# FFT mixing and a gated feed-forward: transfers with 24 rows outermost, radix-2 sums on GpSimd behind the first mix half, and a 72-row matmul for the last groups

## The chip, the cores and the metric

The kernel runs on one core of one Trainium2 chip. The metric is the device time of one launch in microseconds (us). TensorE is called PE, VectorE DVE, ScalarE ACT, GpSimd POOL, and SyncE, which issues almost all transfers of this kernel in order, SP.

## The reference

```python
X = np.fft.rfft(x, axis=1)                      # x: 8 transforms, 3072 points, 256 channels
Yr = Xr @ w_r - Xi @ w_i + b_r                  # complex 256 x 256 mix of each frequency
Yi = Xr @ w_i + Xi @ w_r + b_i
Y = soft_threshold(Yr, 0.01) + 1j * soft_threshold(Yi, 0.01)
y = np.fft.irfft(Y, n=3072, axis=1)             # 24576 tokens of 256
out = ((y @ w_a) * (y @ w_b)) @ w_out           # 256 -> 1536 -> 256
```

## The kernel before

The feed-forward takes most of TensorE's time. It walks over 32 pairs of 384 tokens each way (4 quarters `q` for each of the 8 transforms `b`) and, in each, over 12 steps `j` of the hidden dimension (`step`). A step makes seven products of a Strassen scheme (`ych`, `ycl` with weights `wc`), which ScalarE copies out of PSUM (`s`, L1097; `g`) and VectorE adds up, and then the projection (`g` with `wo`). All operands are split into a high and a low part, so that a product is three matmuls.

Between the matmuls of a step stand two **slots**. A slot takes one task from a list, and the tasks are the Fourier stages of the *next* transform, so that they run in the shadow of the feed-forward:

- **f1** (13 units `u`, in the first quarter): `f1_load` brings a tile `xin` of 5 groups of 24 rows, ScalarE casts it to the high part (`x<-xin`, L469), GpSimd subtracts to get the low part, TensorE multiplies with the constants `c_sb`, ScalarE copies the result out (`gst`, L351), and SP stores it to the scratch `g_d`. `f1_pre` issues the load of unit u+3 and the cast of unit u+2 when unit u runs.
- **f2** (12 units): `mid_load` brings two rows of `g_d` (`gt`); their sum and difference are `gs`; TensorE multiplies them with `m_in`. Then comes a chain that prepares the mix: ScalarE copies (`xs`, L351) and casts (`sx`, L702), GpSimd or VectorE subtracts (`sx`, 512 elements a row), adds (`xs`, 256), ScalarE casts (L705), and GpSimd or VectorE subtracts again (`sx`, 256).
- **f3** (two halves of a unit): the complex mix, `sx` with `wm_h`, `wm_l`. The first half needs the 512-element `sx` at once, the cast L705 at its seventh matmul and the last `sx` at its ninth. Behind the second half VectorE builds `zy` and the clipped `zc`, GpSimd subtracts (`zy`), ScalarE casts (`zh`), GpSimd subtracts (`zl`).
- **i1**: `zh`, `zl` with `v_sb`; ScalarE copies to `dst`, and the sum and difference of its halves, `dto`, are stored to the scratch `d_d`.
- **i2** (four parts a quarter): `i2_load` brings `dt` (5 groups of 24 rows) and, in two of the four parts, `dl` (2 groups of 24, 48 rows); TensorE multiplies them with `t_in`; the results become the `ych`, `ycl` of the next pair of token groups.

The order of a unit's tasks is f3, f3, f2 of the next unit, i1 of the unit before, so four slots, two steps, a unit. `Order` is a planner that keeps model times for the engines and writes each engine's instructions in the order in which the model finds them ready; operations marked "GV" go to GpSimd unless the model finds that much too late, "VG" and "AV" likewise. `need` makes sure that a chain is written before the matmul that reads it. On the chip each engine runs its own list in order. The sum and difference `gs` are written by `mid_load`, `dto` by `i1`, whenever the model finds them ready:

```python
            ready = od.chain(
                ("GV", D, lambda e: tt(e, both[:, 0], t[:, 0], t[:, 1], ALU.add)),
                ("GV", D, lambda e: tt(e, both[:, 1], t[:, 0], t[:, 1], ALU.subtract)),
                after=ready,
            )
```

Of the kernel before, what the change touches and what calls it, by code (L numbers as in the profile page):

```python
# [43 lines left out]
def _constants():  # L44
# [72 lines left out]
    b1h, b1l = _split(b1.reshape(RB, (G + 1) * KT))  # L117
# [22 lines left out]
    b2 = np.zeros((G, KT, NPAIR, 6, G, M1))  # L140
    e2 = np.zeros((2, KT, NPAIR, 2, M1))
    for q in range(NPAIR):
        for h in range(G):
            for j in range(6):
                b2[h, :, q, j, h] = back[32 * q + 6 * h + j]
        for h in range(2):
            e2[h, :, q, h] = back[32 * q + 30 + h]
# [11 lines left out]
        "b1": np.ascontiguousarray(np.stack([b1h, b1l], 1)),  # L159
# [3 lines left out]
        "e2": e2.reshape(2 * KT, NPAIR * 2 * M1).astype(np.float32),  # L163
# [162 lines left out]
def fft_mix_glu_kernel(ctx: ExitStack, tc: tile.TileContext, x, w_r, w_i, b_r, b_i, w_a, w_b, w_out, c1f, vf, m2, v, t2, c3, b1, m2b, vz, b2, e2, out):  # L326
# [45 lines left out]
    c1_sb = const.tile([RB, 2, RB + KT], F32R, name="c1_sb")  # L372
# [53 lines left out]
    def split_mix():  # L426
        w2, w3, v_in = (p1.tile([P, 2, D], F32, tag=t, name="w_in") for t in ("sxh", "sxl", "xs"))
        v_in = v_in.rearrange("p s (i n) -> p s i n", i=2)
        c1_in = state["tmp"].tile([RB, 2, RB + KT], F32, name="c1_in", bufs=1)
# [3 lines left out]
        for q, bq in enumerate((b_r, b_i)):  # L433
# [4 lines left out]
            ("AV", 2 * (RB + KT), lambda e: copy(e, c1_sb, c1_in)),  # L438
# [101 lines left out]
    def out_weights(j):  # L540
# [29 lines left out]
    def f1_load(b, u):  # L570
        if b:
            t = p3.tile([RB, 512], F32, tag="ld", name="xin")
            xv = x[b].rearrange("(p m n) d -> m p (n d)", p=M1, n=2)
            if u < 6:
                nc.sync.dma_start(t, xv[u : u + 4 * STEP + 1 : STEP])
            else:
                nc.sync.dma_start(t[M1:], xv[u : u + 3 * STEP + 1 : STEP])
                nc.sync.dma_start(t[:M1], xv[min(u + 4 * STEP, 63)])
# [6 lines left out]
    def f1_pre(b, u):  # L585
# [6 lines left out]
        xs[b, u] = xh, xl, od.chain(*split(512, xi, xh, xl), after=t if b < 2 else 0.0)  # L592
# [28 lines left out]
    def f1_later(b, u):  # L621
        if u == 0:
            g_d[b] = dram.tile([KT, P * D], F32, tag="g_d", name="g_d")
# [3 lines left out]
        at = KT * (u >= 6)  # L627
        mm3(ps[:RB], c1_sb[:, 0, at : at + RB], c1_sb[:, 1, at : at + RB], xh, xl, True, True)
        g = p2.tile([RB, 512], F32, tag="st", name="gst")
        n = 5 if u + 4 * STEP < 64 else 4  # L630
        to = g_d[b].rearrange("s (m e) -> m s e", e=512)[u : u + (n - 1) * STEP + 1 : STEP]
        c = od.chain(
            ("AV", 512, lambda e: copy(e, g, ps[:RB])),
            ("S", 0, lambda e: nc.sync.dma_start(to, g[: n * KT])),
# [20 lines left out]
    def mid_load(b, u):  # L655
# [8 lines left out]
        ready = od.load(3 * P)  # L664
        both = p3.tile([P, 2, D], F32, tag="ld", name="gs") if u else t
        if u:
            ready = od.chain(
                ("GV", D, lambda e: tt(e, both[:, 0], t[:, 0], t[:, 1], ALU.add)),
                ("GV", D, lambda e: tt(e, both[:, 1], t[:, 0], t[:, 1], ALU.subtract)),
                after=ready,  # L670
            )
        gt[b, u] = both, m, ready

    def f2(b, u):
# [3 lines left out]
        elif u:  # L678
            od.need(t)
# [66 lines left out]

    f3_ps = {}
    zs_done = []

    def f3_plain(u, i):  # L750
# [33 lines left out]
        z = p1.tile([P, 2, D], F32, tag=("zy", "zc")[u % 2], name="zc")  # L784
# [16 lines left out]
    def f3(b, u, i):  # L801
# [17 lines left out]
        if i == 0:  # L819
# [11 lines left out]
            f3_ps[b, u] = bk, k, od.chain(*ops, urgent=1)  # L831
            return
# [369 lines left out]
    with tc.manual_schedule():  # L1202
# [140 lines left out]
```

## Time and profile before

| | |
|---|---|
| runs | 2970.67, 2972.41, 2974.66 us (median 2972.41) |
| profiled execution | 2974.97 us; its span, first to last instruction, 2973.2 us |
| PE | 2878.7 us busy, 97% of the span |
| DVE | 1909.4 us, 64% |
| ACT | 1446.4 us, 49% |
| POOL | 925.7 us, 31% |
| mean granted TensorE clock | 0.990 |
| chain that ended last | PE 75%, DMA 5%, ACT 5%, POOL 4%, issue 3%, DVE 3% |

Matmuls overlap each other in the profile, so a busy PE may still start its matmuls late; the share of the chain is what was followed back from the last instruction. The profiled execution took 2.6 us more than the median of the runs.

### The profile page before, as it was taken

How to read it: one execution, taken by the hardware profiler on the slowest of the kernel's cores; microseconds unless marked ns; L12 is line 12 of the kernel's file. 1: busy time of each engine (PE TensorE's matmuls, PEld its weight loads, DVE VectorE, ACT ScalarE, POOL GpSimd, SP SyncE). 2: the span in 40 equal slices, each digit the busy share in tenths (PEclk: the TensorE clock that was granted, in tenths of full speed). 3: DMA queues.
4: the chain of work that ended last, by engine and by line, in shares of the span. 5: the costliest groups of instructions: out<-in, count | busy, mean ns of one | idle time of the engine just before them, and what ended most of it. 6: DMA issues, size and time to landing. Idle time of an engine off the chain costs nothing.

```text
span 2973.2 us, 47139 instructions
## 1 busy us (share of the span) xinstructions
PE 2878.7 (97%) x16879; PEld 2666.9 (90%) x16879; DVE 1909.4 (64%) x3790; ACT 1446.4 (49%) x3212; POOL 925.7 (31%) x922
## 2 busy tenths in 40 slices
PE   7899999999999999999999999999999999999999
PEld 3589999899989999889998999989999899999998
DVE  7666666566755667556665666656666566666665
ACT  5554445545455444544445454454444544444444
POOL 1123433234422334224333243333342234420000
PEclk8899999999999999999999999999999999999999
DMA  7431212212122011321113111222112211110000
GB/s 244 136 101 41 58 36 83 83 41 62 37 98 81 29 57 40 108 72 41 47 48 110 57 59 33 60 100 59 54 36 63 99 56 56 39 46 27 27 11 22
DMA packets 130596, 190.08 MB, mean 64 GB/s; under 512 B 14389, under 2 KB 87473, under 8 KB 130361
## 3 DMA queue, kind: packets, MB, share of 16 engines
q1 hardware_dynamic: 128409, 179.55, 19.4%
q0 software_dynamic: 1840, 7.48, 0.8%
q8 instruction: 132, 2.16, 0.3%
q14 instruction: 103, 0.84, 0.1%
q10 hardware_dynamic: 112, 0.04, 0.0%
HBM read 111.52 MB, written 75.50 MB: 63 GB/s over the span
## 4 chain that ended last, share of the span: by engine, by line
PE 75%; DMA 5%; ACT 5%; POOL 4%; issue 3%; DVE 3%; SPq 1%; ACTq 0%; POOLq 0%; DVEq 0%
PE bank L360 75%; DMA xin<-in_x_dram 4%; ACT s L1097 2%; POOL sx L354 2%; DVE bank L354 1%; DMA gt<-g_d 1%; POOL gs L354 1%; POOL dto L354 1%; POOL xs L354 1%; DVE s L354 1%; POOL zl L354 0%; ACT x L469 0%; DVE zy L354 0%; ACT ych L469 0%; ACT xs L351 0%
## 5 line engine op out<-in xcount | busy, mean ns | idle before, releaser
L354 DVE TENSOR_TENSOR bank<-bank,s 128x384 f32<-128x384 f32 x1152 | 647.5, 562 | 608.7 <-PE bank L360 493.2
L1097 ACT COPY s<-bank 128x384 f32<-128x384 f32 x1152 | 550.0, 485 | 206.4 <-PE bank L360 202.0
L1134 ACT CAST g<-bank 128x384 fp32r<-128x384 f32 x384 | 184.6, 481 | 808.5 <-DVE s L354 412.3
L354 DVE TENSOR_TENSOR g<-bank,g 128x384 fp32r<-128x384 f32 x768 | 425.6, 556 | 195.3 <-ACT g L1134 158.4
L354 DVE TENSOR_TENSOR s<-bank,s 128x384 f32<-128x384 f32 x768 | 423.0, 551 | 8.4 <-issue 1.0
L354 POOL TENSOR_TENSOR ycl<-yr,ych 128x384 fp32r<-128x384 f32 x186 | 194.8, 1068 | 719.9 <-ACT ych L469 719.9
L1072 ACT CAST g<-bank 128x384 fp32r<-128x384 f32 x384 | 185.0, 482 | 214.5 <-DVE bank L354 213.9
L360 PE MATMUL bank<-ych,wc0l 128*128 128x384 f32 x672 | 237.3, 353 | 17.8 <-ACT s L1097 17.7
L354 POOL TENSOR_TENSOR zy<-zy,zc 128x512 f32<-128x512 f32 x77 | 99.0, 1286 | 468.0 <-DVE zc L850 468.0
L360 PE MATMUL bank<-ych,wc1l 128*128 128x384 f32 x672 | 233.3, 347 | 9.4 <-ACT s L1097 8.8
L360 PE MATMUL bank<-ych,wc3l 128*128 128x384 f32 x672 | 235.5, 351 | 1.4 <-ACT s L1097 1.0
L360 PE MATMUL bank<-ych,wc2l 128*128 128x384 f32 x672 | 235.0, 350 | 1.1 <-DVE s L354 0.9
L354 POOL TENSOR_TENSOR x<-xin,x 120x512 fp32r<-120x512 f32 x88 | 118.0, 1344 | 375.6 <-ACT x L469 213.4
L360 PE MATMUL bank<-ycl,wc0h 128*128 128x384 f32 x672 | 229.2, 341 | 0.0
L360 PE MATMUL bank<-ych,wc0h 128*128 128x384 f32 x672 | 229.1, 341 | 0.0
L360 PE MATMUL bank<-ycl,wc2h 128*128 128x384 f32 x672 | 226.5, 337 | 0.0
L360 PE MATMUL bank<-ycl,wc3h 128*128 128x384 f32 x672 | 226.4, 337 | 0.0
L360 PE MATMUL bank<-ycl,wc1h 128*128 128x384 f32 x672 | 226.3, 337 | 0.0
L360 PE MATMUL bank<-ych,wc1h 128*128 128x384 f32 x672 | 226.2, 337 | 0.0
L360 PE MATMUL bank<-ych,wc2h 128*128 128x384 f32 x672 | 226.2, 337 | 0.0
L360 PE MATMUL bank<-ych,wc3h 128*128 128x384 f32 x672 | 226.1, 336 | 0.0
L360 PE MATMUL bank<-wm_h,sx 128*128 128x256 f32 x1008 | 196.6, 285 | 12.9 <-POOL sx L354 12.8
(210 smaller groups left out, 6699.7 us busy)
## 6 DMA issues: line engine op xcount, KB each, us to landing
out_dram<-osb SPq DMA_DIRECT2D x64, 384.0 KB
g_d<-gst SPq DMA_DIRECT2D x84, 240.0 KB
dt<-d_d SPq DMA_DIRECT2D x56, 360.0 KB
gt<-g_d SPq DMA_DIRECT2D x154, 128.0 KB
d_d<-dto SPq DMA_DIRECT2D x154, 128.0 KB
xin<-in_x_dram SPq DMA_DIRECT2D x65, 192.0 KB
m_in<-const_m2b_dram SPq DMA_DIRECT2D x84, 128.0 KB
xin<-in_x_dram SPq DMA_DIRECT2D x42, 240.0 KB
```

The lines of the kernel that those rows point to most:

```text
L354: (nc.vector if e == "V" else nc.gpsimd).tensor_tensor(o, a, b, op=op)
L360: nc.tensor.matmul(o, lhsT=l, rhs=r, start=start, stop=stop, **kw)
L1072: ("A", W, lambda e: nc.scalar.copy(h, X)),
L1097: return s, od.chain(("A", W, lambda e: nc.scalar.copy(s, q[:, :W])), urgent=1)
L1134: ("A", W, lambda e: nc.scalar.copy(h1, Y)),
```

## The change

Five things are edited. (1) The tiles of f1 and i2 change their row order from (group, row) to (row, group), and the DRAM side of their transfers has the 24 rows as its outermost dimension in place of the 5, 4 or 2 groups; each f1 load is now two transfers in all 13 units, and the row of the scratch `g_d` is padded so that all units store 5 groups. The constants `b1`, `b2`, `e2` are reordered to match. (2) The last groups' matmul takes three groups, 72 rows, the first of which meets zero weights. (3) The sums `gs` of unit u+1 and `dto` of earlier units are written by `halves` directly behind the first mix half of unit u; `zc` shares the buffer of the low part of `sx`. (4) The list of f1 tasks leaves a slot empty after two units, before every third. (5) The cast of an f1 tile is written no earlier than the model's landing time, in all transforms and not in the first two alone.

```diff
-    e2 = np.zeros((2, KT, NPAIR, 2, M1))
+    b2 = np.zeros((KT, G, NPAIR, 6, G, M1))
+    e2 = np.zeros((KT, 3, NPAIR, 2, M1))
...
-            e2[h, :, q, h] = back[32 * q + 30 + h]
+            e2[:, h + 1, q, h] = back[32 * q + 30 + h]
...
-            xv = x[b].rearrange("(p m n) d -> m p (n d)", p=M1, n=2)
-            if u < 6:
-                nc.sync.dma_start(t, xv[u : u + 4 * STEP + 1 : STEP])
-            else:
-                nc.sync.dma_start(t[M1:], xv[u : u + 3 * STEP + 1 : STEP])
-                nc.sync.dma_start(t[:M1], xv[min(u + 4 * STEP, 63)])
+            xv = x[b].rearrange("(p m n) d -> p m (n d)", p=M1, n=2)
+            at, one = (u + STEP, u) if u < 6 else (u, min(u + 4 * STEP, 63))
+            nc.sync.dma_start(t[: 4 * M1], xv[:, at : at + 3 * STEP + 1 : STEP])
+            nc.sync.dma_start(t[4 * M1 :], xv[:, one])
...
-        xs[b, u] = xh, xl, od.chain(*split(512, xi, xh, xl), after=t if b < 2 else 0.0)
+        xs[b, u] = xh, xl, od.chain(*split(512, xi, xh, xl), after=t)
...
-        at = KT * (u >= 6)
-        mm3(ps[:RB], c1_sb[:, 0, at : at + RB], c1_sb[:, 1, at : at + RB], xh, xl, True, True)
+        c1u = c1_sb[:, int(u >= 6)]
+        mm3(ps[:RB], c1u[:, 0], c1u[:, 1], xh, xl, True, True)
         g = p2.tile([RB, 512], F32, tag="st", name="gst")
-        n = 5 if u + 4 * STEP < 64 else 4
-        to = g_d[b].rearrange("s (m e) -> m s e", e=512)[u : u + (n - 1) * STEP + 1 : STEP]
+        to = g_d[b].rearrange("s (h m e) -> s h m e", h=G, e=512)[:, :, u]
         c = od.chain(
             ("AV", 512, lambda e: copy(e, g, ps[:RB])),
-            ("S", 0, lambda e: nc.sync.dma_start(to, g[: n * KT])),
+            ("S", 0, lambda e: nc.sync.dma_start(to, g)),
...
-        ready = od.load(3 * P)
         both = p3.tile([P, 2, D], F32, tag="ld", name="gs") if u else t
-        if u:
-            ready = od.chain(
-                ("GV", D, lambda e: tt(e, both[:, 0], t[:, 0], t[:, 1], ALU.add)),
-                ("GV", D, lambda e: tt(e, both[:, 1], t[:, 0], t[:, 1], ALU.subtract)),
-                after=ready,
-            )
-        gt[b, u] = both, m, ready
+        gt[b, u] = both, m, t
...
-            od.need(t)
+            od.need(state["halves"])
...
             od.put(state["x"])
+            od.put(state["z"], 2 * (u > 1))
...
+    def halves(o, i, *then):
+
+        return od.chain(
+            ("GV", D, lambda e: tt(e, o[:, 0], i[:, 0], i[:, 1], ALU.add)),
+            ("GV", D, lambda e: tt(e, o[:, 1], i[:, 0], i[:, 1], ALU.subtract)),
+            *then,
+        )
...
+            if u < 11:
+                both, _, t = gt[b, u + 1]
+                state["halves"] = halves(both, t)
+            while later:
+                later.popleft()()
...
-        z = p1.tile([P, 2, D], F32, tag="zc", name="zc")
...
+        z = p1.tile([P, 2, D], F32, tag="sxl", name="zc")
...
+        if b and u > 1:
+            od.put(state["dto"])
...
-            ops = [
-                ("AV", 512, lambda e: copy(e, d, ps)),
-                ("GV", D, lambda e: tt(e, to[:, 0], d[:, 0], d[:, 1], ALU.add)),
-                ("GV", D, lambda e: tt(e, to[:, 1], d[:, 0], d[:, 1], ALU.subtract)),
-                ("S", 0, lambda e: mid_move(d_d[b], u, to, True)),
-            ]
-        c = od.chain(*ops, urgent=len(ops) if u == 11 or b == 0 else 1)
-        od.reads(bk, c, len(ops) - 1)
-        if u == 11:
-            (od.put if b else od.need)(c)
+            ops = [("AV", 512, lambda e: copy(e, d, ps))]
+
+            def last():
+                state["dto"] = halves(to, d, ("S", 0, lambda e: mid_move(d_d[b], u, to, True)))
+
+        c = od.chain(*ops, urgent=len(ops))
+        if b == 0 or u == 0:
+            od.reads(bk, c, 1)
+        else:
+            od.reads(bk, c, 0)
+            if u < 10:
+                later.append(last)
+            else:
+                od.put(c)
+                last()
+                if u == 11:
+                    od.put(state["dto"])
+        if b == 0 and u == 11:
+            od.need(c)
...
-        src = dv[:, :30].rearrange("s (h j) d -> h s j d", j=6)[:, :, 3 * th : 3 * th + 3]
+        src = dv[:, :30].rearrange("s (h j) d -> s h j d", j=6)[:, :, 3 * th : 3 * th + 3]
         nc.sync.dma_start(
-            t.rearrange("p n d -> p (n d)"), src.rearrange("h s j d -> h s (j d)")
+            t.rearrange("p n d -> p (n d)"), src.rearrange("s h j d -> s h (j d)")
         )
         cut = [(t[:, n], m[:, n * RB : (n + 1) * RB]) for n in range(3)]
         if th == 0:
-            last = p2.tile([2 * KT, D], F32, tag="dl", name="dl")
-            nc.sync.dma_start(m[: 2 * KT, T3:], e2[:, 2 * KT * q : 2 * KT * (q + 1)])
-            nc.sync.dma_start(last, dv[:, 30:].rearrange("s h d -> h s d"))
-            cut.append((last, m[: 2 * KT, T3:]))
+            last = p2.tile([3 * KT, D], F32, tag="dl", name="dl")
+            nc.sync.dma_start(m[: 3 * KT, T3:], e2[:, 2 * KT * q : 2 * KT * (q + 1)])
+            nc.sync.dma_start(last, dv[:, 29:])
+            cut.append((last, m[: 3 * KT, T3:]))
...
-                        work += f1_tasks(b + 1)[0 if b else AHEAD :]
+                        ts = f1_tasks(b + 1)[0 if b else AHEAD :]
+                        for i in range(0, len(ts), 3):
+                            work += [*ts[i : i + 2], None, *ts[i + 2 : i + 3]]```

GpSimd's list at the beginning of a transform's third quarter, from the fifth unit's `zy` to the last `sx` of the sixth unit, in the kernel before (a row is an operation, its tiles and its shape):

```order
L354 TENSOR_TENSOR zy<-zy,zc 128x512
L354 TENSOR_TENSOR zl<-zy,zh 128x512
L354 TENSOR_TENSOR gs<-gt 128x256
L354 TENSOR_TENSOR sx<-xs,sx 128x2x256
L354 TENSOR_TENSOR gs<-gt 128x256
L354 TENSOR_TENSOR xs<-xs 128x2x128
L354 TENSOR_TENSOR sx<-xs,sx 128x2x128
```

The `gs` in it belong to a later unit. The same place in the changed kernel, from the sums behind the fifth unit's first mix half:

```order
L355 TENSOR_TENSOR gs<-gt 128x256
L355 TENSOR_TENSOR dto<-dst 128x256
L355 TENSOR_TENSOR gs<-gt 128x256
L355 TENSOR_TENSOR dto<-dst 128x256
L355 TENSOR_TENSOR zy<-zy,zc 128x512
L355 TENSOR_TENSOR zl<-zy,zh 128x512
L355 TENSOR_TENSOR sx<-xs,sx 128x2x256
L355 TENSOR_TENSOR xs<-xs 128x2x128
L355 TENSOR_TENSOR sx<-xs,sx 128x2x128
```

Nothing stands between `zl` and the last `sx` any more but the chain itself, and the four sums stand ahead of `zy`. The 42 `xs` and 35 last `sx` that VectorE did are now GpSimd's, as are all 154 `gs` and all 154 `dto`. In one unit of each transform a `ycl` stands between `xs` and the last `sx`, and in one five `ycl` stand ahead of the sums.

SP's list in the f1 stage of the kernel before (a store of `g_d`, then the two transfers of a load; the shape is that of the written side):

```order
L634 DMA g_d<-gst 5x24x512
L577 DMA xin<-in_x_dram 96x1x512
L578 DMA xin<-in_x_dram 24x512
L634 DMA g_d<-gst 5x24x512
L577 DMA xin<-in_x_dram 96x1x512
L578 DMA xin<-in_x_dram 24x512
```

The 96-row load reads 4 groups of 24 rows here. The same stretch of SP's list in the changed kernel:

```order
L632 DMA g_d<-gst 120x512
L576 DMA xin<-in_x_dram 96x1x512
L577 DMA xin<-in_x_dram 24x512
L632 DMA g_d<-gst 120x512
L576 DMA xin<-in_x_dram 96x1x512
L577 DMA xin<-in_x_dram 24x512
```

The order is the same; the store is one dimension of 120 rows, and the read side of the 96-row load, which these rows don't print, is 24 rows of 4 groups.

## Rows read from the trace of the kernel before

**Rows 1.** The page, busy time, share and instructions of each engine.
```profile
PE 2878.7 (97%) x16879; PEld 2666.9 (90%) x16879; DVE 1909.4 (64%) x3790; ACT 1446.4 (49%) x3212; POOL 925.7 (31%) x922
```

**Rows 2.** Windows: stretch, length, busy us (count) by engine, clock, DMA share, GB/s.
```profile
2676.00:2736.00 60.00, 59.73 (x344) 56.29 (x343) 37.67 (x71) 27.24 (x61) 1.99 (x2) 1.00 0.10 33
869.00:929.00 60.00, 56.81 (x303) 51.47 (x301) 28.20 (x54) 30.84 (x66) 12.73 (x10) 0.97 0.31 111
...
sum 423.00, PE 394.10 PEld 356.15 DVE 208.70 ACT 218.46 POOL 100.10; mean PE 56.30 PEld 50.88 DVE 29.81 ACT 31.21 POOL 14.30
```

**Rows 3.** ACT's waits, window 1230 to 1290: us in total, times, longest.
```profile
ACT x L469 <- DMA xin<-in_x_dram: 10.0, 8, 2.4
```

**Rows 4.** Timelines of ACT and PE at 1247: start, us, what, idle before.
```profile
1247.64 0.62 ACT L469 CAST x<-xin 120x512 fp32r<-120x512 f32 x1 [1.20 <-DMA xin<-in_x_dram]
...
1248.69 0.44 PE L360 MATMUL bank<-ych,wc0l 128*128 128x384 f32 x1 [1.28 <-ACT s L1097]
```

**Rows 5.** The chain that ended last: start, us from issue to landing.
```profile
875.65 8.34 DMA xin<-in_x_dram
1418.46 2.86 DMA gt<-g_d
```

**Rows 6.** PE's timeline around i2: 48-row `dl`, then 96-row `dl`.
```profile
915.78 0.83 PE L360 MATMUL bank<-t_in,dt 120*128 120x120 f32 x6
916.53 0.42 PE L360 MATMUL bank<-t_in,dl 48*128 48x48 f32 x2
...
917.10 0.40 PE L360 MATMUL bank<-g,wo5h 128*128 128x256 f32 x2
...
187.83 0.81 PE L360 MATMUL bank<-t_in,dt 96*128 96x96 f32 x6
...
188.85 0.40 PE L360 MATMUL bank<-g,wo4h 128*128 128x256 f32 x2
```

**Rows 7.** Groups by form: shapes xcount | busy us, mean ns | idle before.
```profile
L360 PE MATMUL bank<-t_in,dl 48*128 48x48 f32 x112 | 23.4, 290 | 0.0
L354 POOL TENSOR_TENSOR xs<-xs 128x256 f32<-128x256 f32 x42 | 31.0, 738 | 11.8 <-DVE x L716 11.2
L354 DVE TENSOR_TENSOR xs<-xs 128x256 f32<-128x256 f32 x42 | 28.2, 672 | 0.0
L354 POOL TENSOR_TENSOR sx<-xs,sx 128x256 fp32r<-128x256 f32 x49 | 38.2, 780 | 19.8 <-ACT sx L705 19.6
L354 DVE TENSOR_TENSOR sx<-xs,sx 128x256 fp32r<-128x256 f32 x35 | 15.1, 432 | 0.0
```

**Rows 8.** Timelines of POOL, then PE, around a unit's first mix half.
```profile
1419.48 1.29 POOL L354 TENSOR_TENSOR zl<-zy,zh 128x512 fp32r<-128x512 f32 x1 [2.36 <-ACT zh L469]
1421.44 0.74 POOL L354 TENSOR_TENSOR gs<-gt 128x256 f32<-128x256 f32 x1 [0.67 <-DMA gt<-g_d]
1422.14 1.30 POOL L354 TENSOR_TENSOR sx<-xs,sx 128x512 fp32r<-128x512 f32 x1
...
1423.65 0.28 PE L360 MATMUL bank<-wm_l,sx 128*128 128x256 f32 x1
1424.12 0.40 PE L360 MATMUL bank<-wm_h,sx 128*128 128x256 f32 x2
1425.49 0.38 PE L360 MATMUL bank<-wm_l,sx 128*128 128x256 f32 x1 [0.98 <-ACT sx L705]
1426.30 0.39 PE L360 MATMUL bank<-wm_h,sx 128*128 128x256 f32 x1 [0.31 <-POOL sx L354]
```

**Rows 9.** Waits over the whole span: us in total, times, longest.
```profile
PE bank L360 <- POOL sx L354: 12.8, 31, 0.7
PE bank L360 <- ACT sx L705: 7.2, 7, 1.1
PE bank L360 <- ACT s L1097: 27.4, 51, 1.7
...
POOL zy L354 <- DVE zc L850: 468.0, 77, 7.9
```

More of the change, by code (lines that the diff above doesn't have):

```diff
@@ L116, in _constants @@
         b1[row, :, col] = u1[g]
-    b1h, b1l = _split(b1.reshape(RB, (G + 1) * KT))
+    b1 = np.concatenate([b1[1:].transpose(1, 0, 3, 2).reshape(4 * M1, KT, G + 1), b1[0].transpose(0, 2, 1)])
+    b1h, b1l = _split(np.stack([b1[:, :, i : i + G].reshape(RB, RB) for i in range(2)], 1))
     mt = m2.reshape(KT, 2, N2, P)
@@ L139, in _constants @@
         back[:, 2 * t], back[:, 2 * t + 1] = 2 * np.cos(ang) / S, -2 * np.sin(ang) / S
-    b2 = np.zeros((G, KT, NPAIR, 6, G, M1))
-    e2 = np.zeros((2, KT, NPAIR, 2, M1))
+    b2 = np.zeros((KT, G, NPAIR, 6, G, M1))
+    e2 = np.zeros((KT, 3, NPAIR, 2, M1))
     for q in range(NPAIR):
@@ L144, in _constants @@
             for j in range(6):
-                b2[h, :, q, j, h] = back[32 * q + 6 * h + j]
+                b2[:, h, q, j, h] = back[32 * q + 6 * h + j]
         for h in range(2):
-            e2[h, :, q, h] = back[32 * q + 30 + h]
+            e2[:, h + 1, q, h] = back[32 * q + 30 + h]
     c3 = np.zeros((2, 3, P), np.float32)
@@ L158, in _constants @@
         "c3": c3,
-        "b1": np.ascontiguousarray(np.stack([b1h, b1l], 1)),
+        "b1": np.ascontiguousarray(np.stack([b1h, b1l], 2)),
         "m2b": np.ascontiguousarray(pairs.reshape(KT, P, P).transpose(1, 0, 2)).astype(np.float32),
@@ L162, in _constants @@
         "b2": b2.reshape(RB, NPAIR * 6 * RB).astype(np.float32),
-        "e2": e2.reshape(2 * KT, NPAIR * 2 * M1).astype(np.float32),
+        "e2": e2.reshape(3 * KT, NPAIR * 2 * M1).astype(np.float32),
     }
@@ L369, in mm3 @@
         mm(o, *third, False, stop, **kw)
-    c1_sb = const.tile([RB, 2, RB + KT], F32R, name="c1_sb")
+    c1_sb = const.tile([RB, 2, 2, RB], F32R, name="c1_sb")
     v_sb = const.tile([P, 2, 2, P], F32R, name="v_sb")
@@ L428, in split_mix @@
         v_in = v_in.rearrange("p s (i n) -> p s i n", i=2)
-        c1_in = state["tmp"].tile([RB, 2, RB + KT], F32, name="c1_in", bufs=1)
+        c1_in = state["tmp"].tile([RB, 2, 2, RB], F32, name="c1_in", bufs=1)
         wr, wi = (state["wab"][0][:, :, D * k : D * (k + 1)] for k in range(2))
@@ L437, in split_mix @@
             ("VG", 512, lambda e: tt(e, w2, wi, wr, ALU.subtract)),
-            ("AV", 2 * (RB + KT), lambda e: copy(e, c1_sb, c1_in)),
+            ("AV", 4 * RB, lambda e: copy(e, c1_sb, c1_in)),
         ]
@@ L554, in out_weights @@
             a = p1.tile([P, 2, D], F32, tag="zy", name="wo_a")
-            b = p1.tile([P, 2, D], F32, tag="zc", name="wo_b")
-            hi, lo, w = a[:, 0], a[:, 1], b[:, 0]
+            b = p1.tile([P, D], F32, tag="k", name="wo_b")
+            hi, lo, w = a[:, 0], a[:, 1], b
         ops = [*decode(D, raw, hi, lo, w), *split(D, w, *wo[j])]
@@ L622, in f1_later @@
         if u == 0:
-            g_d[b] = dram.tile([KT, P * D], F32, tag="g_d", name="g_d")
+            g_d[b] = dram.tile([KT, 2 * G * STEP * D], F32, tag="g_d", name="g_d")
         xh, xl, c = xs.pop((b, u))
@@ L647, in mid_move @@
         if u:
-            a = t[2 * u : 2 * u + 2].rearrange("c (g n d) -> c n g d", g=2, d=D)
+            a = t[2 * u : 2 * u + 2, : P * D].rearrange("c (g n d) -> c n g d", g=2, d=D)
             parts = [(a[c], tile_[N2 * c : N2 * (c + 1)]) for c in range(2)]
         else:
-            parts = [(t[0:2].rearrange("c (n d) -> n c d", d=D), tile_)]
+            parts = [(t[0:2, : P * D].rearrange("c (n d) -> n c d", d=D), tile_)]
         for a, s in parts:
@@ L745, in f2_plain @@
         xs[0, u] = X, Z, c
+    def halves(o, i, *then):
[4 more added lines that the diff above has]
+        )
     f3_ps = {}
     zs_done = []
+    later = deque()
     def f3_plain(u, i):
@@ L783, in f3_plain @@
         y = state["tmp"].tile([P, 2, D], F32, tag="v", name="zy")
-        z = p1.tile([P, 2, D], F32, tag=("zy", "zc")[u % 2], name="zc")
+        z = p2.tile([P, 2, D], F32, tag="zl", name="zc")
         lo, hi = slice(0, 64), slice(64, 128)
@@ L1281, in fft_mix_glu_kernel @@
                     if more:
-                        work += f1_tasks(b + 1)[0 if b else AHEAD :]
+                        ts = f1_tasks(b + 1)[0 if b else AHEAD :]
+                        for i in range(0, len(ts), 3):
+                            work += [*ts[i : i + 2], None, *ts[i + 2 : i + 3]]
                     else:
```

## The prediction

> **What bounds the kernel now.** I read the page first: PE is busy for 2878.7 of 2973.2 us, the other engines for two thirds at most [rows 1]. So time is saved where PE starts a matmul late, or where a matmul costs more than its columns. I looked for both by stage.
>
> *The f1 stage.* Windows show where PE rests. A stretch of the last transform, with no Fourier tasks, has 59.73 us of PE in 60. The seven stretches that hold f1, 63 us once and 60 us six times, have 394.10 in 423: 28.9 us of rest, against 7 x 0.27 = 1.9 for seven stretches like the last. In them the DMA share is 0.31 (0.10 without f1) and in most the granted clock is 0.97, not 1.00 [rows 2]. 0.31 is 5 of 16 DMA engines busy without a break. The waits name the path: in one such stretch ACT waits 10.0 us in 8 pieces for `xin` [rows 3], and since ACT runs its list in order, the copy `s` behind that cast comes late and PE waits 1.28 us for it [rows 4]. The chain of waits gives the transfer's length: 8.34 us for an `xin`, where a transfer of 64 rows (`gt`) took 2.86 [rows 5].
>
> *The mix.* Over the whole span PE waits 12.8 us in 31 pieces for GpSimd's `sx` and 7.2 us in 7 pieces for ACT's [rows 9]. One place shows both: GpSimd waits 0.67 us for a `gt` that only a `gs` needs, the `sx` of the next mix stands behind that `gs`, and PE's mix stops twice, for 0.98 and 0.31 us [rows 8]. Without stops the nine matmuls from 1423.65 take 8 x 0.1175 us (the fifth starts 0.47 after the first), so the ninth is due at 1424.59. It starts at 1426.30: 1.71 us are lost where 1.29 are shown as idle, a factor of 1.33, since the pipeline also runs empty and the next weights come late.
>
> *The last groups.* From the first `dt` matmul to the second `wo` matmul that follows takes 1.32 us with a 48-row `dl` between and 1.02 us with a 96-row `dl`, twice as wide [rows 6]. Fewer columns cost more. The rows differ in the number of rows, 48 against 96, and I take that for the cause.
>
> **The change part by part.**
>
> *72 rows.* 112 passes, two a matmul, are 56 matmuls [rows 7]. 1.32 - 1.02 = 0.30 us each gives 16.8. The 96-row case has narrower `dt`, which is worth a few hundredths at most against us: I take **-16.5 us**. All 56 stand in PE's own stream. Lower bound: none gained, if 72 rows behave as 48 do; upper bound 17.
>
> *24 rows outermost, empty slots, later casts.* The transfers of f1 lay on 5 DMA engines; with 24 rows outermost the same bytes can lie on more of them. The rest in the seven stretches above that of the last is 28.9 - 1.9 = 27.0 us as shown, and 27.0 x 1.33 = 36 with the restarts. A load is needed by ACT two f1 tasks after it is issued. In the old list that is two slots, one step; in the new list a third of the slots stay empty, 13 units take 18 slots, so each load has about 1.4 times as long. If the landing also falls from 8.34 us to near the 2.86 of `gt` [rows 5], ACT's wait is covered twice over. What covers the 18 slots is the quarter itself, which has 24; the four i2 tasks then stand in slots 18 to 21. I take **-35 us**. Lower end 17 (half, if only the empty slots help), upper end 45, with the low clock in five of the seven stretches (3% of 60 us, 1.8 each) given back on top of 36.
>
> The Trainium skill (DMA: Bandwidth & Descriptors, the section on why a DMA increments its semaphore by 16) says that a transfer uses the largest number up to 16 that divides the slowest dimension of both sides. By that rule the loads go from 5 or 4 engines to 12 and the store from 5 to 15, which gives the whole -35; the share of 0.31 agrees with its 5.
>
> The other transfers with the new order (`dt`, `dl`) are issued a quarter ahead; PE's waits show none for them in this part, so I cost them at nothing. 42 loads become two transfers instead of one; SP has room for these, half a microsecond each.
>
> *Sums behind the first half.* In the new list of GpSimd nothing stands in the chain `zl`, `sx`, `xs`, last `sx`. With the durations of the worst place: `zl` ends at 1420.77, `sx` 1.30 later (1422.07), `xs` 0.74 (1422.81), ACT's cast about 0.4 (1423.3 with a handover), last `sx` 0.78 (1424.1) [rows 7, 8]. PE needs the cast at its seventh matmul, 1424.35, and the last `sx` at its ninth, 1424.59: both are there with about half a microsecond to spare. One unit a transform has a `ycl` in between, and is about even. The seven first units keep their wait of about 0.43 us, since theirs is VectorE's work on the real part, which doesn't move. (12.8 + 7.2 - 7 x 0.43) x 1.33 = 22.6: I take **-22 us**. Lower end 0, if the chain on GpSimd is late everywhere; upper end 27.
>
> Where the sums go: four of some 0.74 to 0.93 us, 3.4 us together, ahead of `zy`. There GpSimd waits for VectorE's `zc` now, 468.0 us in 77 pieces, 6.1 each [rows 9], and the sums fit in. Behind them are queued `zy`, `zl`, the chain above and f2's own read of `gs`, two steps' worth of slots later.
>
> The new place costs something: `xs` takes 738 ns on GpSimd against 672 on VectorE, the last `sx` 780 against 432 [rows 7], 0.41 us a unit longer if both move. I put it at nothing because it lies in the half microsecond counted above; without that cover it would be 77 x 0.41 = 32 us. The Trainium skill (GPSIMD Engine Reference, Engine selection) says the same against this part: elementwise work belongs on VectorE, GpSimd being about two times slower. The rows agree for the last `sx` (1.8 times) and not for `xs` (1.1); by the rule's factor for both, the chain would be 0.67 + 0.43 = 1.10 us longer, 0.6 past the margin, 77 x 0.6 = 46 us, and the sum 2949.
>
> *New waits.* The i2 tasks of the first quarter come later, close to its end, and the copies and splits that follow crowd ACT. I count one more wait of the mean size for `s`, 27.4 / 51 = 0.54 us [rows 9], a transform: **+4 us**. Constants that are a little larger load at the start, beside many others: nothing.
>
> **Sum.** -16.5 - 35 - 22 + 4 = -69.5. The profiled execution took 2974.97, so 2905.5; the median of the runs was 2.6 lower, so **2903 us**.
>
> **Rivals.**
>
> *GpSimd's chain becomes the late one.* The mix is released by three GpSimd operations in a row where VectorE did two of them in half of the units. For it: 0.41 us more a unit against a margin of half a microsecond. Against: GpSimd is free of sums there. If the mix part gains nothing: 2903 + 22 = 2925.
>
> *The loads stay long.* The written side of the 96-row load is as before, and if it decides, the transfers still lie on few engines. Then only the empty slots help: 2903 + 18 = 2921.
>
> *72 rows cost what 48 do.* No row shows 72. 2903 + 16.5 = 2919.5.
>
> *Slower.* The sums hold up f2. In the new list they are the only producers of `gs`, and everything of the unit stands behind them on GpSimd. In one unit of each transform five `ycl` stand ahead of them. I put a `ycl`, 384 elements a row, at 1.0 us, between the 0.74 of 256 and the 1.30 of 512 [rows 8]; 5.0 + 3.4 us is more than the 6.1 us of room, and `zy` is late by 2.3. If that happened in every unit, and each of the 77 lost more than 69.5 / 77 = 0.9 us, the kernel would be slower; at 2.3 us it would be 2903 + 177 = 3080. Against: it is one unit of eleven.
>
> *It does nothing.* PE's late starts move to another engine's wait, and only the matmul's 16.5 stays or not even that: ACT is idle for half its time and VectorE for a third [rows 1], so I see no such engine.
>
> **How the numbers follow.** All three parts pay: 0.66, by itself 2887 (all upper ends: 45 + 27 + 17 - 4 = 85 off 2972) to 2920 (17 of the f1 and mix parts missing). Mix part fails: 0.12. Loads stay long: 0.10. 72 rows: 0.05. Slower: 0.04. Nothing: 0.03. The range goes from 2887 to 2930, past the 2925 and 2921 of the first two rivals, and leaves less than 2 in 10 outside. A measurement of this kernel can tell about 0.2%, 6 us, from no change: faster 0.94, same 0.02, slower 0.04.
>
> **What would show it.** In the changed profile: the DMA share in the f1 stretches lower or its transfers short, no wait of ACT for `xin` above a few us in all, and PE above 59 in 60; the span from `dt` to the second `wo` matmul at about 1.0 us with a 72-row `dl`; PE's waits for `sx` down to the first units' 3 us; the clock at 1.00 there. I am wrong if GpSimd's `xs` or last `sx` ends most of PE's waits, if `gs` begins to, or if ACT still stands at the cast of `xin`.

## The result and the profile after

The changed kernel took 2894.03 us (median, 2890.21 to 2894.30) against 2973.53 for the kernel before: a ratio of 0.973, 95% interval 0.9714 to 0.9747. It is faster by 79.5 us, where 69.5 were predicted; 2903 was forecast, with a range of 2887 to 2930. The profiled execution took 2894.15 us, its span is 2892.4.

The page's first row, which answers to [rows 1]:

```profile
PE 2837.1 (98%) x16879; PEld 2647.5 (92%) x16879; DVE 1853.7 (64%) x3696; ACT 1449.2 (50%) x3212; POOL 970.3 (34%) x1016
```

PE is busy 41.6 us less and idle 39.2 us less (94.5 before, 55.3 now). POOL has 45 us more to do and DVE 56 less: VectorE gave up its `xs` and last `sx` (43.3 us, [rows 7]) and its share of `gs` and `dto` (30.0 us), and took over a few of the subtractions of f1 and i2 (`x`, `ycl`).

Windows of the stretches with f1, columns as in [rows 2]:

```profile
141.00:204.00 63.00, 62.06 (x340) 57.99 (x341) 46.36 (x109) 35.94 (x82) 17.33 (x18) 0.96 0.38 109
...
1200.00:1260.00 60.00, 60.00 (x339) 56.04 (x339) 32.87 (x62) 33.02 (x70) 11.64 (x9) 1.00 0.34 99
...
sum 423.00, PE 422.06 PEld 394.20 DVE 243.42 ACT 234.54 POOL 87.23; mean PE 60.29 PEld 56.31 DVE 34.77 ACT 33.51 POOL 12.46
```

The 28.9 us of rest are 0.9 now, and outside the first stretch the clock is 1.00. The DMA share did not fall (0.34 against 0.31): what changed is its pattern. Here are the DMA engines, in tenths of their time, in 40 slices of 1.5 us of the third transform's f1 stretch, of the changed kernel and then of a kernel with the old f1 transfers (e4_f1_back, below):

```profile
DMA  6874266620164066630064053300050050000066
```
```profile
DMA  3377333332332322333323333223131120026610
```

A constant 3 (a share of 0.31 is 5 of 16 engines) became bursts of up to 8 with empty slices between. The semaphore records of the trace say the same. From the start of its issue to its last increment, an f1 load took 7.2 us (120 rows) or 8.5 us (96 rows) before, and its 96-row part takes 3.7 now (medians); the store took 7.3 and takes 2.4. A load in five groups had 6 increments and one in four groups 5; the parts of a load have 13 each now, and the store 16 where it had 6 or 5.

PE's waits, for [rows 9]:

```profile
PE bank L361 <- ACT s L1114: 8.9, 31, 0.6
PE bank L361 <- POOL sx L355: 5.3, 14, 0.5
...
PE bank L361 <- DVE g L355: 3.8, 6, 0.6
```

The wait for ACT's second `sx` (7.2 us) is gone, that for `s` is a third, that for GpSimd's `sx` less than half. The last row is new. PE never waits for a `gs`. ACT's wait for `xin`, in the kernel before

```profile
ACT x L469 <- DMA xin<-in_x_dram: 64.9, 50, 2.9
```

over the whole span, is not in ACT's list any more.

GpSimd, ACT and PE at the mix of [rows 8], the same unit in the changed kernel:

```profile
1376.41 1.29 POOL L355 TENSOR_TENSOR zl<-zy,zh 128x512 fp32r<-128x512 f32 x1 [2.36 <-PE bank L361]
1377.66 1.29 POOL L355 TENSOR_TENSOR sx<-xs,sx 128x512 fp32r<-128x512 f32 x1
1379.03 0.74 POOL L355 TENSOR_TENSOR xs<-xs 128x256 f32<-128x256 f32 x1
1380.59 0.74 POOL L355 TENSOR_TENSOR sx<-xs,sx 128x256 fp32r<-128x256 f32 x1 [0.81 <-ACT sx L697]
1381.29 0.74 POOL L355 TENSOR_TENSOR gs<-gt 128x256 f32<-128x256 f32 x1
...
1379.73 0.48 ACT L1114 COPY s<-bank 128x384 f32<-128x384 f32 x1 [0.28 <-PE bank L361]
1380.10 0.41 ACT L697 CAST sx<-xs 128x256 fp32r<-128x256 f32 x1
...
1380.57 0.28 PE L361 MATMUL bank<-wm_l,sx 128*128 128x256 f32 x1
...
1381.39 0.40 PE L361 MATMUL bank<-wm_h,sx 128*128 128x256 f32 x2
```

The nine matmuls run from 1380.57 to 1381.52 (the second of the last pair) without a stop, 0.95 us, where they took 2.65. The last `sx` ends at 1381.33: 0.19 us of the half microsecond of spare time that the prediction counted are left. The rest went at ACT, where the cast between `xs` and the last `sx` stands behind a copy `s`: 0.81 us pass there, and 0.49 were counted.

### The profile page after: what moved, and what is told of

The parts are those of the page before. It is cut to its first block, busy times and chain, and to the rows that moved or that the text cites. A ratio compares the mean times of both kernels' runs of the same rounds, so it can differ in the third digit from the quotient of the medians.

```text
span 2892.4 us, 47285 instructions
## 1 busy us (share of the span) xinstructions
PE 2837.1 (98%) x16879; PEld 2647.5 (92%) x16879; DVE 1853.7 (64%) x3696; ACT 1449.2 (50%) x3212; POOL 970.3 (34%) x1016
## 3 DMA queue, kind: packets, MB, share of 16 engines
q1 hardware_dynamic: 132588, 180.81, 21.6%
## 4 chain that ended last, share of the span: by engine, by line
PE 89%; ACT 2%; issue 1%; DVE 1%; POOL 1%; DVEq 0%; POOLq 0%; ACTq 0%
PE bank L361 89%; ACT s L1114 1%; DVE bank L355 1%; POOL xs L355 0%; POOL sx L355 0%; POOL ycl L355 0%; DVE yr L355 0%; ACT xs L352 0%; ACT sx L694 0%; DVE s L355 0%; ACT g L1089 0%; ACT osb L352 0%; DVE sp L707 0%; ACT dst L352 0%; DVE g L355 0%
## 5 line engine op out<-in xcount | busy, mean ns | idle before, releaser
L355 DVE TENSOR_TENSOR bank<-bank,s 128x384 f32<-128x384 f32 x1152 | 648.6, 563 | 625.5 <-PE bank L361 505.7
L1114 ACT COPY s<-bank 128x384 f32<-128x384 f32 x1152 | 551.6, 484 | 208.0 <-PE bank L361 199.7
L355 DVE TENSOR_TENSOR g<-bank,g 128x384 fp32r<-128x384 f32 x768 | 426.3, 557 | 176.6 <-ACT g L1151 148.2
L355 DVE TENSOR_TENSOR s<-bank,s 128x384 f32<-128x384 f32 x768 | 424.0, 552 | 9.6 <-issue 0.8
L355 POOL TENSOR_TENSOR ycl<-yr,ych 128x384 fp32r<-128x384 f32 x174 | 187.6, 1102 | 671.8 <-ACT ych L470 671.4
L361 PE MATMUL bank<-ych,wc0l 128*128 128x384 f32 x672 | 234.1, 348 | 7.3 <-ACT s L1114 5.1
L361 PE MATMUL bank<-ych,wc3l 128*128 128x384 f32 x672 | 236.2, 351 | 3.3 <-ACT s L1114 2.7
L355 POOL TENSOR_TENSOR x<-xin,x 120x512 fp32r<-120x512 f32 x82 | 106.5, 1299 | 380.7 <-ACT x L470 380.7
L361 PE MATMUL bank<-ych,wc2l 128*128 128x384 f32 x672 | 233.2, 347 | 0.0
L361 PE MATMUL bank<-ych,wc1l 128*128 128x384 f32 x672 | 231.7, 345 | 1.2 <-ACT s L1114 1.2
L361 PE MATMUL bank<-ycl,wc0h 128*128 128x384 f32 x672 | 227.6, 339 | 0.1
L361 PE MATMUL bank<-ych,wc0h 128*128 128x384 f32 x672 | 227.5, 339 | 0.0
L361 PE MATMUL bank<-ycl,wc2h 128*128 128x384 f32 x672 | 227.1, 338 | 0.0
L361 PE MATMUL bank<-ycl,wc3h 128*128 128x384 f32 x672 | 227.0, 338 | 0.0
L361 PE MATMUL bank<-ycl,wc1h 128*128 128x384 f32 x672 | 226.6, 337 | 0.0
L361 PE MATMUL bank<-ych,wc2h 128*128 128x384 f32 x672 | 226.6, 337 | 0.0
L361 PE MATMUL bank<-ych,wc3h 128*128 128x384 f32 x672 | 226.6, 337 | 0.0
L361 PE MATMUL bank<-ych,wc1h 128*128 128x384 f32 x672 | 226.5, 337 | 0.0
L355 POOL TENSOR_TENSOR zy<-zy,zc 128x512 f32<-128x512 f32 x77 | 98.9, 1284 | 361.2 <-DVE zc L856 361.2
L355 POOL TENSOR_TENSOR sx<-xs,sx 128x512 fp32r<-128x512 f32 (+1 forms) x168 | 170.5, 1015 | 86.4 <-ACT sx L697 53.1
```

What stands on the lines that cost most here:

```text
L355: (nc.vector if e == "V" else nc.gpsimd).tensor_tensor(o, a, b, op=op)
L361: nc.tensor.matmul(o, lhsT=l, rhs=r, start=start, stop=stop, **kw)
L1114: return s, od.chain(("A", W, lambda e: nc.scalar.copy(s, q[:, :W])), urgent=1)
```

## The experiments

Medians of 4 or 5 runs, beside runs of the kernel before on the same chip (2972.97 to 2975.77). "After the start" is the span less the start of the 918th matmul, which begins a long unbroken piece of PE in the chain of waits; everything ahead of it is the first transform's stages and the first f1 stretch.

| kernel | us | ratio to before, interval | start | after the start |
|---|---|---|---|---|
| before | 2973.53 | | 252.61 | 2720.6 |
| changed | 2894.03 | 0.9730, 0.9714 to 0.9747 | 242.50 | 2649.9 |
| e1_sums_back | 2912.41 | 0.9799, 0.9785 to 0.9812 | 237.10 | 2671.5 |
| e12_gs_alone | 2896.50 | 0.9739, 0.9725 to 0.9752 | 239.55 | 2656.4 |
| e4_f1_back | 2933.50 | 0.9871, 0.9857 to 0.9884 | 249.74 | 2682.3 |
| e9_late_casts_only | 2937.39 | 0.9874, 0.9860 to 0.9887 | 251.84 | 2683.5 |
| e3_groups_outer_f1 | 2903.70 | 0.9768, 0.9755 to 0.9781 | 249.92 | 2654.6 |
| e2_no_empty_slots | 2886.58 | 0.9712, 0.9699 to 0.9725 | 239.86 | 2644.3 |
| e8_fewer_empty | 2887.98 | 0.9705, 0.9690 to 0.9721 | 239.00 | 2647.1 |
| e11_early_casts | 2887.98 | 0.9707, 0.9694 to 0.9720 | 243.32 | 2642.8 |
| e10_mix_on_vector | 2891.04 | 0.9719, 0.9706 to 0.9732 | 243.84 | 2646.7 |
| e5_48_rows | 2910.15 | 0.9780, 0.9766 to 0.9793 | 241.10 | 2667.2 |
| e6_64_rows | 2909.81 | 0.9781, 0.9768 to 0.9794 | 238.10 | 2667.2 |
| e13_72_rows_alone | 2957.51 | 0.9941, 0.9928 to 0.9955 | 252.71 | 2706.3 |

The start varies between 237 and 244 us among kernels whose work there is nearly the same, so differences of up to some 5 us between medians are read from the last column.

For f1 that column leaves something out, since part of the start is f1's too. From the 351st matmul, the first of the third f1 unit, to the 918th, the five kernels with the old f1 transfers took 112.0 to 114.9 us and the nine with the new ones 103.9 to 106.2. The scatter lies ahead of the 351st matmul (133.1 to 139.4 us). Counted from there, the changed kernel is faster than the one before by 79.9 us, and undoing a part costs 21.6 (e1), 41.0 (e4) or 17.3 us (e5). Both columns come from one profiled execution of each kernel.

### The sums

```diff
# e1_sums_back
-            if u < 11:
-                both, _, t = gt[b, u + 1]
-                state["halves"] = halves(both, t)
-            while later:
-                later.popleft()()
+        if u:   # in mid_load; dto likewise in i1's chain
+            ready = od.chain(
+                ("GV", D, lambda e: tt(e, both[:, 0], t[:, 0], t[:, 1], ALU.add)),
...
```

> The changed kernel with the sums gs and dto back in the chains of mid_load and i1; everything else as changed. My step (the sums behind the first mix half are worth 22 us, 26 with the f1 part then the rest): slower than the changed kernel by 20 to 27 us, 2914 to 2921, and PE waits again about 10 us for GpSimd's sx and some for ACT's. Rival, that the f1 part gained more than the 35 us I gave it and the sums little: slower by 5 us or less, 2899.

It is 18.4 us slower by the medians, less than the 20 to 27 expected, and 21.6 after the start. GpSimd in e1_sums_back, the same unit as above:

```profile
1381.40 1.30 POOL L355 TENSOR_TENSOR zl<-zy,zh 128x512 fp32r<-128x512 f32 x1 [2.36 <-ACT zh L470]
1383.22 0.74 POOL L355 TENSOR_TENSOR gs<-gt 128x256 f32<-128x256 f32 x1 [0.53 <-DMA gt<-g_d]
1383.92 1.29 POOL L355 TENSOR_TENSOR sx<-xs,sx 128x512 fp32r<-128x512 f32 x1
```

The `gs` stands between `zl` and `sx` again and waits for its `gt`. PE's waits in the same kernel are those of before:

```profile
PE bank L361 <- POOL sx L355: 11.8, 30, 0.7
...
PE bank L361 <- ACT sx L704: 6.8, 7, 1.1
```

In e12_gs_alone only `dto` goes back to i1's chain (`halves` keeps the `gs`):

> The changed kernel with only the sums dto back in the chain of i1; the sums gs stay behind the first mix half. With both back it took 2912.4, 18.4 more than the changed kernel. If the gs were what stood in the way of the mix, as the place that I read in the trace had it: 2894 to 2899. If dto delays the mix as much as gs: 2903. If dto alone does: 2912.

2896.50, 2.5 us slower (6.5 after the start): PE waits 28 times for GpSimd's `sx`, but 8.9 us in all and never for ACT's. The `gs` are about three quarters of the part, `dto` the rest.

### The f1 part

```diff
# e4_f1_back: all three; e9_late_casts_only: the first and the last; e3_groups_outer_f1: the first
-            xv = x[b].rearrange("(p m n) d -> p m (n d)", p=M1, n=2)
+            xv = x[b].rearrange("(p m n) d -> m p (n d)", p=M1, n=2)
...
-        xs[b, u] = xh, xl, od.chain(*split(512, xi, xh, xl), after=t)
+        xs[b, u] = xh, xl, od.chain(*split(512, xi, xh, xl), after=t if b < 2 else 0.0)
...
-                        ts = f1_tasks(b + 1)[0 if b else AHEAD :]
-                        for i in range(0, len(ts), 3):
-                            work += [*ts[i : i + 2], None, *ts[i + 2 : i + 3]]
+                        work += f1_tasks(b + 1)[0 if b else AHEAD :]
```

> The changed kernel with the whole f1 part undone: groups outermost, no empty slots, the casts written early; the sums and the 72 rows stay. By the sum of my prediction it is slower than the changed kernel by 35 us, 2929; since the whole change gained 12 us more than predicted, up to 45, 2939, if the surplus belongs to f1. If the surplus belongs to the sums: 30 to 35.

> The changed kernel with f1's transfers groups outermost and its tasks in consecutive slots, as before, and only the late casts kept. Beside the run with early casts as well (2933.5) and the one with the empty slots as well (2903.7). If the empty slots gained the 30 us between these two: 2930 to 2934. If the late casts gained them (ACT and PE no longer stand behind a cast whose load is still under way): 2904 to 2910.

> The changed kernel with the transfers of f1 (loads, stores and their constants) groups outermost again, 5 or 4 groups by 24 rows; i2, the empty slots and the later casts stay. Theory A (the layout carries the f1 part): slower by 18 us or more, 2912 or above, loads that land after about 8 us, ACT waiting for xin. Theory B (the empty slots carry it): within 5 us of the changed kernel, 2889 to 2899, though the loads take as long as before.

> The changed kernel with the f1 tasks in consecutive slots again; the layout and the later casts stay. Theory A (the shorter landing of the loads alone covers ACT's wait): within 5 us of the changed kernel, 2889 to 2899, ACT's wait for xin a few us at most. Theory B (the empty slots carry at least half of the f1 part, as the rival in which the loads stay long has it): slower by 17 us or more, 2911 or above, with PE near 56 or 57 in 60 in the f1 stretches.

e4 is 39.5 us slower than the changed kernel, within its range. e3 is 9.7 us slower, which is neither theory: both edits carry a part. e9 is slower still than e4, 3 us above the range in which the empty slots gain the 30 us, so the late casts don't. e2 is 7.4 us faster than the changed kernel, 2.4 below the range of theory A; theory B falls.

The layout and the slots make a table of four (late casts in all):

| | consecutive slots | every third empty |
|---|---|---|
| groups outermost | 2937.4 (e9) | 2903.7 (e3) |
| 24 rows outermost | 2886.6 (e2) | 2894.0 (changed) |

The layout alone gains 50.8 us. The empty slots alone gain 33.7, though the loads take nearly as long as before (8.1 us for 96 rows); but on top of the layout they lose 7.4 (5.6 after the start). From the 351st matmul on the three are about 47, 31 and a loss of 4. Either edit acts on the same wait: PE's wait for `s` is 34.2 us in e9, 13.9 in e3 and 9.0 in e2. ACT's wait for `xin` in e9, in e3 and in e2:

```profile
ACT x L469 <- DMA xin<-in_x_dram: 67.9, 51, 3.1
```
```profile
ACT x L469 <- DMA xin<-in_x_dram: 34.4, 30, 2.6
```
```profile
ACT x L470 <- DMA xin<-in_x_dram: 5.9, 5, 2.2
```

In e3 the chain of waits still has one `xin` a transform (start, us):

```profile
859.50 7.41 DMA xin<-in_x_dram
1213.75 7.77 DMA xin<-in_x_dram
```

The late casts gain nothing: 2937.4 with them and 2933.5 without in the old layout, and in the new one the kernel without empty slots took 2886.6 with them and 2888.0 without (e11_early_casts: the line with `after=t if b < 2 else 0.0` added to e2_no_empty_slots); after the start these two took 2644.3 and 2642.8. That is the second case of what was expected:

> The changed kernel without the empty slots and with the casts of f1 written early again, as before the change. With the old transfers the late casts made it 3.9 us slower (2937.4 against 2933.5). If that is a property of the casts' place: 2883. If late casts only matter where a load is late, they do nothing with loads of some 3 us: 2884 to 2889. If an early cast makes ACT stand for a load again: 2890 or more, with a wait of ACT for xin above 6 us.

Why the empty slots cost: in the changed kernel PE stops once near the end of most transforms' first quarter (PE, start, us, idle before):

```profile
921.93 0.51 PE L361 MATMUL bank<-g,wo10h 128*128 128x512 f32 x1 [0.63 <-DVE g L355]
```

DVE is late there since it stood at an i2 result (`yr`, behind GpSimd's `ycl`):

```profile
920.05 1.35 DVE L355 TENSOR_TENSOR yr<-yr 128x384 f32<-128x384 f32 x1 [0.95 <-POOL ycl L355]
921.33 0.55 DVE L355 TENSOR_TENSOR g<-bank,g 128x384 fp32r<-128x384 f32 x1
```

```diff
# e8_fewer_empty
-                        for i in range(0, len(ts), 3):
-                            work += [*ts[i : i + 2], None, *ts[i + 2 : i + 3]]
+                        for i in range(0, len(ts), 6):
+                            work += [*ts[i : i + 5], None, *ts[i + 5 : i + 6]]
```

> The changed kernel with one empty slot after every five f1 units in place of one after every two, so that f1 takes 15 slots and not 18 and the i2 tasks come three slots earlier. If the empty slots cost time because they push i2 to the end of the quarter, where its copies and additions crowd with the next pair's (PE's wait for VectorE's g there, six times 0.6 us): 2885 to 2889, with that wait gone. If they cost time by themselves, or the quarter's end isn't the place: 2891 to 2895, with the wait still there.

2887.98: the wait for DVE's `g` is gone from PE's list, as it is in e2. The edit leaves three of the five empty slots, so f1 takes 16 slots and i2 comes two slots earlier, not three. Only 2.8 of the 6.0 us stand after the start, and PE's wait for `s` grew from 8.9 to 11.1 us (38 times). The place of the wait is confirmed, and half of e2's 5.6 us come back; what the other half is was not shown.

### The 72 rows

```diff
# e5_48_rows (with its constants)
-            last = p2.tile([3 * KT, D], F32, tag="dl", name="dl")
-            nc.sync.dma_start(last, dv[:, 29:])
+            last = p2.tile([2 * KT, D], F32, tag="dl", name="dl")
+            nc.sync.dma_start(last, dv[:, 30:])
# e6_64_rows
-            cut.append((last, m[: 3 * KT, T3:]))
+            cut.append((last[:64], m[:64, T3:]))
```

> The changed kernel with the last groups' matmul on 48 rows again (two groups, their own constants, a 48-row transfer); the order of all instructions on TensorE, VectorE, ScalarE and GpSimd is the same. My step: 56 matmuls lose 0.30 us each, 16.5 in all, so 2911. Rival (72 rows cost what 48 do): 2894.

> The changed kernel with 64 of the 72 rows in the last groups' matmul; it leaves out the last 8 rows of the sum, all else (the transfers too) is the same. If a matmul of at most 64 rows is the dear kind: 2911, like 48 rows. If the cost falls with the rows, from 0.30 us at 48 to nothing at 72: a third of it, about 2900. If 48 rows are dear for a reason of their own (their transfer, their number): 2894.

> The kernel before with nothing but the 72 rows in the last groups' matmul (its transfer groups outermost, as before). If the saving is TensorE's own, 0.29 us for each of 56 matmuls whatever else waits: 16 us faster than before, 2958. If it is hidden behind the waits of the kernel before: 2965 to 2974.

PE's timeline at the same i2 task with 72 rows (changed), 48 (e5) and 64 (e6); the row behind `dl` is the next product:

```profile
902.84 0.82 PE L361 MATMUL bank<-t_in,dt 120*128 120x120 f32 x6
903.50 0.33 PE L361 MATMUL bank<-t_in,dl 72*128 72x48 f32 x2
903.64 0.42 PE L361 MATMUL bank<-ych,wc3l 128*128 128x384 f32 x1
```
```profile
904.64 0.82 PE L361 MATMUL bank<-t_in,dt 120*128 120x120 f32 x6
905.40 0.42 PE L361 MATMUL bank<-t_in,dl 48*128 48x48 f32 x2
905.75 0.44 PE L361 MATMUL bank<-ych,wc3l 128*128 128x384 f32 x1
```
```profile
901.57 0.82 PE L361 MATMUL bank<-t_in,dt 120*128 120x120 f32 x6
902.33 0.42 PE L361 MATMUL bank<-t_in,dl 64*128 64x48 f32 x2
902.67 0.44 PE L361 MATMUL bank<-ych,wc3l 128*128 128x384 f32 x1
```

From the first `dt` to the product: 0.80, 1.11 and 1.10 us. So 72 rows save 0.31 us, 17.4 for 56; the medians say 16.1 with the part undone (17.3 after the start, in e5 and e6 alike) and 17.1 with it alone. The profiled execution of e13, the slowest of its five, has 14.3 after the start, with PE idle for 5.6 us longer than in the kernel before. 64 rows cost what 48 do: it is no slope with the number of rows, but a step between 64 and 72, and the transfer has no part in it, since e6 moves 72 rows.

### The mix on VectorE

```diff
# e10_mix_on_vector, on e2_no_empty_slots
-            ("GV", 256, lambda e: tt(e, xs_, xs_, xsf[:, :, P:], ALU.add)),
+            ("VG", 256, lambda e: tt(e, xs_, xs_, xsf[:, :, P:], ALU.add)),
...
-            ("GV", 256, lambda e: tt(e, xl[:, :, 2], xs_, xhf[:, :, 2], ALU.subtract)),
+            ("VG", 256, lambda e: tt(e, xl[:, :, 2], xs_, xhf[:, :, 2], ALU.subtract)),
```

> The changed kernel without the empty slots (2886.6) and with xs and the last sx offered to VectorE first. PE's 14 waits for GpSimd's sx, 5.2 us, times 1.33 is 7 us at most. Theory (that chain is half on GpSimd for want of a choice, and the shorter operations on VectorE, 0.41 us a unit, end the waits): 2880 to 2883. Rival (VectorE's list is the fuller one, 64% against 34%, and the two operations stand behind its sums there or delay them): 2887 to 2900, with PE waiting for VectorE's s or g.

2891.04, 4.5 us above e2 (2.5 after the start). PE's 14 waits for GpSimd's `sx` became these:

```profile
PE bank L361 <- DVE sx L355: 4.5, 7, 0.7
```

The total hardly moved, but the places did. The seven first units' waits of 0.30 us are gone, so there the engine was the cause; in the seven units with a `ycl` the wait grew from 0.45 to 0.64 us, and the kernel as a whole got no faster. The theory that the engine is the cause of all 14 falls, and not all that was expected of the rival came (PE's wait for DVE's `s` is 2.1 us, 1.7 in e2).

## Why the prediction was right, point by point

**72 rows** (-16.5): right in size and in kind, with 16.1 and 17.1 measured. The reason given, the number of rows, holds as a step.

**Sums** (-22): 18.4 by medians, 21.6 after the start. The mechanism is the one read from [rows 8]; that the size fits so well is in part luck, since two errors cancel. Fewer waits went than the 17.0 us counted: 13.3 between e1 (11.8 + 6.8) and the changed kernel (5.3). But each microsecond of them was worth 1.6, or 1.5 without e1's one dip of the clock, and not the 1.33 taken from a single place. The spare half microsecond at the ninth matmul was 0.19, so seven units, those with a `ycl` in between, kept a wait of about 0.45 us beside the seven first units' 0.30: 5.3 us of waits where 3.0 were counted. The waits that are left come to 5.3 us in 14 units, not to half a microsecond in each of 77. That the first units' wait is VectorE's work and doesn't move was wrong: it fell from 0.43 to 0.30 us, and in e10 it is gone. The rival in which the sums hold up `zy` did not come: GpSimd still waits for VectorE's `zc`, 361.2 us in 77 pieces, so the room was there. The rule that spoke against this part (the Trainium skill, GPSIMD Engine Reference, Engine selection: elementwise work belongs on VectorE) would have given 2949. In e10, which follows it for these two operations, they are shorter (626 ns for `xs` and 464 for the last `sx` on VectorE, against 769 and 737 on GpSimd in the changed kernel), and the kernel is 4.5 us slower than e2.

**The f1 part** (-35, and +4 of new waits): 39.5 by medians, 41.0 from the 351st matmul on, against 31. This is the term that was mis-sized, by nearly all of the 10 us by which the sum was short, and its reasoning on the empty slots was wrong. The range held because its upper end had room for this.
- Its size: PE's waits for `s` and `gst` that go from e4 to the changed kernel are 22.3 and about 6 us, less the 3.8 for `g`: 24.5, times 1.33 is 33. What the value left out, and put in the upper end alone, is the clock. Windows of the kernel before around four of its five dips between 250 and 2900 us, then of e4's two (the clock column is the mean of a window that lies partly at 2.4 GHz, the full clock, and partly at 1.2):

```profile
884.00:892.00 8.00, 6.86 (x27) 6.25 (x28) 3.61 (x7) 3.88 (x8) 2.57 (x2) 0.79 0.33 122
1062.00:1070.00 8.00, 7.04 (x35) 6.57 (x36) 3.06 (x7) 1.75 (x4) 1.08 (x2) 0.79 0.00 0
1608.00:1616.00 8.00, 6.74 (x29) 6.11 (x28) 3.52 (x7) 3.80 (x8) 2.57 (x2) 0.79 0.34 122
1970.00:1978.00 8.00, 7.12 (x29) 6.57 (x30) 3.79 (x7) 3.99 (x8) 2.57 (x2) 0.79 0.33 121
```
```profile
1940.00:1948.00 8.00, 7.52 (x26) 6.21 (x24) 2.15 (x4) 3.54 (x8) 2.07 (x2) 0.57 0.33 123
2294.00:2302.00 8.00, 6.36 (x26) 5.41 (x25) 2.86 (x6) 3.65 (x7) 1.50 (x3) 0.79 0.34 125
```

  A dip costs at most (1 - 0.79) x 8 = 1.7 us, five of them 8.4; e4's two cost at most 3.4 + 1.7 = 5.1. The changed kernel has none there. 33 + 5.1 = 38 of the 39.5. That the dips belong to the stops is argued from their places, not tried by itself: each lies where PE had been stopping, but the stops around 1248 us in the kernel before, its most crowded ones, have none, and e13, which kept the stops of the kernel before, has one dip, twice as long, where that has five. So how many dips a kernel gets could not have been summed beforehand.
- The empty slots were priced as half of the gain where they stand alone, and rightly taken to cover the same wait as the layout; that they would then only cost was not drawn from it. "What covers the 18 slots is the quarter itself" failed: beside the layout they are a loss of 4 to 7 us, by where one counts from. The +4 for new waits was right in place and size (3.8 us of idle), but it was put down to ACT's `s` and is VectorE's `g`, and it is the part of the empty slots' price that could be placed.
- "Loads stay long", the rival in which only the slots help, was under-priced as to the slots: e3 is that case, and it took 2903.70 where the rival had 2921.
- Of the sign "the DMA share lower or its transfers short" only the second half came. The rule on the slowest dimension (the Trainium skill, DMA: Bandwidth & Descriptors, the section on why a DMA increments its semaphore by 16) gives 5 and 4 engines for the loads before, 12 for those after and 15 for the store; the records agree, with one increment more each time (6, 5, 13 and 16).

**The sum.** Undone one by one, the parts are 16.1 + 18.4 + 39.5 = 74.0 of 79.5 by medians. Without the scatter ahead of the 351st matmul they are 17.3 + 21.6 + 41.0 = 79.9, all of the 79.9 that the change gains there. So the parts don't overlap, and next to nothing is left for the edits that no run undid by themselves: the new order of `dt` and `dl` and the shared buffer of `zc`.

The best version tried is the change without empty slots: 2886.58 us, 0.9712 (0.9699 to 0.9725). e8 and e11 cannot be told from it.

## What to carry to other kernels

When two edits of one change answer the same wait, price each alone and then the second on top of the first: here either took away most of what PE lost by it, and with the layout in place the empty slots brought only their own cost. A stop on TensorE cost 1.3 to 1.6 times its idle time here, so take that factor from several places and not from one. Keep the dips of the clock that the windows show as a bound of their own: they lay behind stops, but their number was not that of the stops. Look for matmuls of at most 64 rows between taller ones, which can be padded with zero weights.

## What the runs showed of the hardware

- The step between 64 and 72 rows: 0.31 us for each two-pass matmul, 0.10 ahead of the `dl` row and 0.21 between it and the next product. The Trainium skill (TensorEngine Tiling (Array Packing), Key Properties and Available Configurations) has it that a change of tiling mode drains the engine, and lists modes of 64 and of 128 rows. That 48 and 64 rows behave alike and 72 rows cost nothing extra among the 120 agrees with this, and 0.31 us would be the price of going there and back; no run here shows that these matmuls run in such a mode.
- Nearly the same data in bursts over more engines, at a share of 0.34, served this kernel better than a constant 0.31: what counted was the time of one load, 3.7 us against 7.2 and 8.5. The mean share alone doesn't show the difference.
- The first 917 matmuls took 237 to 244 us in kernels with the new layout. The difference lies ahead of the 351st, which began at 133.1 to 138.4 us, with clocks of 0.66 to 0.76 between 30 and 60 us (the mean up to the 351st was 0.92 in e2, where that took 134.1 us, and 0.87 in the changed kernel, 138.4); no edit tried here explains it.
